# Moving a weight sum, four output copies and a pair of sums in a fused mLSTM and gated feed-forward kernel

## The chip, the cores and the metric

The kernel runs on one core of a Trainium2 chip. The metric is the device time of one execution in microseconds (us). The kernel before takes 461.69 us, the median of three runs that lie between 461.58 and 464.37.

The engines are named as the profile names them: PE is TensorE's matmul, PEld its weight load, DVE is VectorE, ACT is ScalarE, POOL is GpSimd and SP is SyncE, which here only issues DMAs. DMAs are also issued from ACT's queue and, for one chunk, from POOL's.

## The reference

An mLSTM cell with 4 batches, 8 heads, 768 time steps and a head size of 40 is followed by a feed-forward block over the 3072 tokens, from 320 to 2048 and back to 320, all in float32:

```
for t in range(S):
    m_new = np.maximum(f_gate[:, :, t] + m, i_gate[:, :, t])
    f_stab = np.exp(f_gate[:, :, t] + m - m_new)
    i_stab = np.exp(i_gate[:, :, t] - m_new)
    m = m_new
    C = f_stab[:, :, None, None] * C + i_stab[:, :, None, None] * np.einsum('bhd,bhe->bhde', vt, kt)
    n = f_stab[:, :, None] * n + i_stab[:, :, None] * kt
    h_tilde = np.einsum('bhde,bhe->bhd', C, qt)
    nq = np.einsum('bhd,bhd->bh', n, qt)[:, :, None]
    y[:, :, t] = sigmoid(o_gate[:, :, t]) * h_tilde / np.maximum(np.abs(nq), 1.0)
x = y.transpose(0, 2, 1, 3).reshape(B * S, H * D)
h = x @ w_in
g = h * (1.0 / (1.0 + np.exp(-1.702 * h)))
out = g @ w_out
```

(`vt`, `kt` and `qt` are the step's slices of v, k and q, and `sigmoid` stands for the expression written out.)

## The kernel before

**Chunks and stages.** The 768 steps are cut into six chunks of 128 (`w` = 0 to 5). A chunk's tokens are those of all four batches, 512 in all. For each chunk there is a first product (x by `w_in`, then the gate function) and a second product (by `w_out`). While the second product of chunk w runs on PE, the attention of chunk w + 1 is computed in between, block by block, so that its x is there when PE ends. Attention works on two halves, `c` = 0 and 1, of two batches each.

**The order of work is written out by hand.** There is no scheduler: each engine runs its instructions in the order in which the code issues them, and waits on semaphores where it reads what another engine or a DMA wrote.

**Fast products.** From chunk 1 on both products use a scheme with seven block products instead of eight, which needs sums of weights and of inputs. `weight_sums(0)` to `(3)` (line 811) make the sums of `w_out` once, on POOL, in place of room that chunk 0 used; sums 0 and 1 are issued at the end of chunk 0, sums 2 and 3 during the first product of chunk 1. `wait_for(x)` (line 596) is a copy of one column on POOL, whose only purpose is that POOL waits until `x` is written. `input_sums` (lines 673 to 676) make the sums of `w_in` on DVE, in two parts, after blocks 11 and 13 of chunk 0. `token_sums` (lines 684 to 689) make those of x on DVE, ahead of each fast first product.

**Chunk 0's second product** (`down`, line 798) is plain: 16 blocks of four products each, whose sums stay in four PSUM banks, one a batch. After blocks 9, 11, 13 and 15 a batch is complete: its bank is copied to `o_sb` (line 802) and stored by SP (line 803).

**The second product of chunks 1 to 5** (`down_fast`) has 14 blocks, 0 to 6 for the first half of the batches and 7 to 13 for the second. Each block is eight matmul pairs (line 852), and DVE copies or adds its bank to the outputs (lines 855 and 857). The last block of a half, and its third, read `total(2)`, a sum of gated inputs; between the two `last_sums` (line 837) changes each of its four parts in place on DVE. Parts 0 and 1 are changed behind the third block; parts 2 and 3 in the fifth block, ahead of that block's adds. In the last block the first four matmul pairs read parts 0 and 1, the others 2 and 3. Store 1 of a half goes to SP behind the sixth block's add, store 0 behind the last.

**Attention beside these blocks**, for the next chunk: weights (ACT line 439, POOL masks line 443), the state's carry (PE line 605, which needs `k_st`; DVE lines 583 and 616; POOL lines 592 and 583), scores (PE line 463, DVE line 466), values (PE lines 507 and 515) and `outputs` on DVE: lines 521 and 522, the denominator `den` (lines 473 to 475), and the gated outputs y (lines 477 and 482). `seam_out` writes y of a half to DRAM (`x_row` and `x_rest`, line 560; from SP for the first half, from ACT's queue for the second), `seam_in` fetches it back into `q_sq` (line 569, SP), and `seam_turn` transposes it into xT on DVE (line 576). Text below calls the transposes of the first half turn 0 and those of the second turn 1.

**Loads.** All inputs of a chunk are fetched one or two chunks ahead, in SP's queue: the squares of k and q (line 108) at block 13 (k) and 15 (q) of chunk 0 and at block 13 of later chunks, the gates' rows (lines 304 to 354), the weights' rows (line 407), and v and k (line 120). One DMA queue carries them in the order of issue.

Of the kernel before, what the change touches and what calls it, by code (L numbers as in the profile page):

```python
# [26 lines left out]
def kernel(  # L27
# [42 lines left out]
    V, A, G, T = nc.vector, nc.scalar, nc.gpsimd, nc.tensor  # L70
# [7 lines left out]
    t1, t2, t4 = (t_sb[:, i, :].rearrange("p (f m) -> p f m", m=DH) for i in range(3))  # L78
# [31 lines left out]
    def load(w, what, bs=slice(0, B)):  # L110
        hs = slice(bs.start * H, bs.stop * H)
        for c in what:
            if c == "o" and w not in eo:
                eo[w] = ld.tile([L, BH, D], FP, tag="eo", bufs=1, name="eo")
            dst, src = {"k": (k_of(w), k), "q": (q_st, q), "v": (v_st, v), "o": (eo.get(w), o_gate)}[c]
            if w and c in "kv":
                for i, t, r in ((0, slice(0, L), slice(0, L)), (1, slice(0, HL), slice(HL, L)),
                                (1, slice(HL, L), slice(0, HL))):
                    x = src[:, :, w * L + t.start:w * L + t.stop, :].rearrange("b (p two) s d -> two s (b p) d", two=2)
                    nc.sync.dma_start(out=dst[r, i::2, 0:D], in_=x[i])  # L120
                continue
            nc.sync.dma_start(out=dst[:, hs, 0:D],
                              in_=src[bs, :, w * L:(w + 1) * L, :].rearrange("b h s d -> s (b h) d"))
# [103 lines left out]
    kT, qT, ys, xT, gs, o_ps, sums, vw, x_row = {}, {}, {}, {}, {}, {}, {}, {}, {}  # L227
# [366 lines left out]
    def wait_for(x):  # L594

        G.tensor_copy(out=mark[0:x.shape[0]], in_=x[:, 0:1])
# [196 lines left out]
    def down(w, b, n):  # L793
        if n == 0:
            o_ps[w, b] = ps_m.tile([128, DM], FP, tag="m", name="p_out")
        po = o_ps[w, b]
        for f in range(n * 4, n * 4 + 4):
            T.matmul(po, gs[w, f // 2][:, f % 2, b * L:(b + 1) * L], w_out_sb[:, f, :], start=(f == 0),  # L798
                     stop=(f == NF - 1))
        if n == NF // 4 - 1:  # L800
            o = op.tile([128, DM], FP, tag="o", name="o_sb")
            V.tensor_copy(out=o, in_=po)
            nc.sync.dma_start(out=out[b * S + w * L:b * S + (w + 1) * L, :], in_=o)


# [3 lines left out]
    def weight_sums(n):  # L809
        out, a, b = ((t1, w01, w00), (t2, w11, t1), (w01, w11, w01), (t4, w10, t2))[n]  # L810
        G.tensor_tensor(out=out, in0=a, in1=b, op=OP.subtract)

    def hidden(w, j, b):

        return gs[w, j].rearrange("p i (c two t) -> p i c two t", two=2, t=L)[:, :, :, b, :]

    def hidden_difference(w, j):

        a00, a10 = hidden(w, j, 0), hidden(w, j, 1)
        G.tensor_tensor(out=a10, in0=a00, in1=a10, op=OP.subtract)  # L820
# [12 lines left out]
    def last_sums(w, c, js):  # L833

        for j in js:
            s2 = sums[w, 2, j // 2][:, j % 2, :, c]
            V.tensor_tensor(out=s2, in0=hidden(w, j + 4, 0)[:, :, c], in1=s2, op=OP.subtract)

    def down_fast(w, c):
        o = [op.tile([128, DM], FP, tag="o", name="o_sb") for _ in range(2)]  # L840
        o00, o01, o10, o11 = (o[i][:, n * DH:(n + 1) * DH] for i in range(2) for n in range(2))

        def block(two, k):
            return lambda f: gs[w, k * 4 + f // 2][:, f % 2, (2 * c + two) * L:(2 * c + two + 1) * L]

        def total(x):
            return lambda f: sums[w, x, f // 4][:, f // 2 % 2, f % 2, c, :]

        def product(a, b, *adds):
            po = ps_m.tile([128, DH], FP, tag="m", name="p_out")  # L850
            for f in range(NH):
                T.matmul(po, a(f), b[:, f, :], start=(f == 0), stop=(f == NH - 1))  # L852
            for dst, x in adds:
                if x is None:
                    V.tensor_copy(out=dst, in_=po)
                else:
                    V.tensor_tensor(out=dst, in0=x, in1=po, op=OP.add)  # L857

        def store(two):
            b = 2 * c + two  # L860
            nc.sync.dma_start(out=out[b * S + w * L:b * S + (w + 1) * L, :], in_=o[two])

        return [lambda: product(block(0, 0), w00, (o11, None)),
                lambda: product(block(0, 1), w10, (o00, o11)),
                lambda: (product(total(2), t2, (o01, o11)), last_sums(w, c, (0, 1))),
                lambda: product(block(1, 0), w01, (o10, o01)),
                lambda: (last_sums(w, c, (2, 3)), product(total(1), t1, (o11, o10), (o01, o01))),
                lambda: (product(block(1, 1), t4, (o10, o10)), store(1)),
                lambda: (product(total(2), w11, (o01, o01)), store(0))]


    def run(calls):
        for f, *args in calls:
            f(*args)
# [62 lines left out]
    for w in range(NW):  # L937
        more = w + 1 < NW
        if w == 0:
            for j in range(NF // 2):  # L940
                if j % 2 == 0:
                    ahead, behind = converted[j // 2]
                    run([(convert, p) for p in ahead] + [(fetch, p) for p in fetched.get(j // 2, ())])
                    up(w, j, lambda: run([(columns_turn, 1) if p is None else (convert, p) for p in behind]))
                if j == 6:
                    load(1, "o")
                if j == 1:
                    wait_for(w_in_sb[:, 1, 512:1024])
                    scale(0, 1)
                    load(1, "v")  # L950
                if j < B and j % 2:
                    carry(0, (j // 2,))
                if j == 3:
                    masks()
                    gates(1)
                    columns_in(1)
                if j == 4:
                    spread(1)
                    load_squares(1, "q")
                if j >= B:  # L960
                    transposes(1, j - B)
        else:
            token_sums(w)
            for j in range(NF // 2):
                up_fast(w, j)
                if more and j == 0:
                    gates(w + 1)
                    load(w + 1, "o")
                    if w == 1:
                        wait_for(ends[w + 1])  # L970
                if w == 1 and j < 2:
                    weight_sums(j + 2)
                if more and j == 2:
                    columns_in(w + 1)
                    spread(w + 1)
                    load(w + 1, "vk")
                if more and j:
                    for n in ((0, 2), (), (4,), (6, 1, 3), (5, 7), (), ())[j - 1]:
                        block_transposes(w + 1, n)
                if more and j == 7:  # L980
                    columns_turn(w + 1)
                if 2 <= j < 6:
                    hidden_difference(w, j - 2)
                if j >= 6:
                    hidden_sums(w, (j - 6,), G)
            gelu_fast(w, NF // 2 - 1)
            hidden_sums(w, (2, 3), V)
        side = attention(w + 1) if more else {}
        if w == 0:

            blocks = [(lambda b=b, n=n: down(w, b, n)) for n0 in (0, 2) for b in range(B) for n in (n0, n0 + 1)]
        else:
            blocks = down_fast(w, 0) + down_fast(w, 1)
        for i, block in enumerate(blocks):
            if w == 0 and i in (0, 4, 5):
                convert((17, 18, 19)[max(i - 3, 0)])
            if w + 2 < NW and i == (6 if w == 0 else 0):
                load_gates(w + 2)
            if w + 2 < NW and i == 13:
                load_squares(w + 2, "kq" if w else "k")  # L1000
            if w == 0 and i == 15:
                load_squares(w + 2, "q")
            block()
            run(side.get(i, []))
            if w == 0 and i == 3:
                for n in (1, 3, 5, 7):
                    block_transposes(1, n)
            if w == 0 and i == 6:
                wait_for(wt[1, 0][:, 0, 0, :])
                weight_sums(0)  # L1010
                weight_sums(1)
            if w == 0 and i in (11, 13):
                input_sums(slice(0, 4) if i == 11 else slice(4, 8))
# [30 lines left out]
```

## Time and profile before

| | |
|---|---|
| median of three runs | 461.69 us |
| the profiled execution, its time | 463.3 us |
| its span, first to last instruction | 461.6 us |
| PE busy | 452.8 us (98%) |
| PEld busy | 386.5 us (84%) |
| DVE busy | 350.9 us (76%) |
| ACT busy | 186.0 us (40%) |
| POOL busy | 162.7 us (35%) |
| mean granted TensorE clock | 1.000 |
| DMA | 52.87 MB, mean 115 GB/s |

The profile is of one execution, whose own time lies above its span by what is done before the first and after the last instruction. A row of a view in order of time has the start, the duration in us, the engine, the line of the code, the operation, what it writes and reads, its shape and the number of instructions merged; in brackets stands the idle time before it and what ended it. Where a row merges several instructions its duration is that of all of them. Instructions overlap a little at their ends, and matmuls, which are pipelined, more. Of the page's costliest groups these matter for the change:

```profile
L857 DVE TENSOR_TENSOR o_sb<-o_sb,p_out 128x160 f32<-128x160 f32 x70 | 21.4, 317 | 43.6 <-PE p_out L852 43.0
L768 ACT COPY parts<-p_h 128x256 f32<-128x256 f32 x40 | 14.9, 372 | 164.6 <-PE p_h L729 159.5
```

The columns are: line, engine, operation, out<-in, shapes and count; busy us and mean ns of one; idle time of the engine before them and what ended most of it. Two groups that the page leaves out are of interest too: `last_sums` (line 837) is 40 instructions of 609 ns on average, but 397 to 1505 each, and the copy of line 802 four instructions of 480 to 495 ns. `weight_sums` (line 811) is four instructions of some 2.9 us on POOL.

### The profile page before, as it was taken

To read this page: it belongs to the slowest core of one execution; us is meant where nothing else is said; L and a number is where in the kernel's file an instruction comes from. 1 tells how busy PE (TensorE), PEld (TensorE's weight loads), DVE (VectorE), ACT (ScalarE), POOL (GpSimd) and SP (SyncE) were. 2 spreads that over 40 slices of the span, in tenths; PEclk is the share of its full clock that TensorE was granted. 3 is DMA by queue.
4 is the path that set the end of the run, shared out by engine and by line. 5 is a ranking of instruction groups with operands and counts; after the bars stand their busy time and mean duration, and the time that the engine had idled before them with its cause. 6 is when DMAs were issued, how large, how long until landed. Compare 5 with 4: busy or idle time off the path is not lost.

```text
span 461.6 us, 12375 instructions
## 1 busy us (share of the span) xinstructions
PE 452.8 (98%) x5071; PEld 386.5 (84%) x5071; DVE 350.9 (76%) x738; ACT 186.0 (40%) x433; POOL 162.7 (35%) x155
## 2 busy tenths in 40 slices
PE   8999999999999999999899999999999999999996
PEld 6777877775779999779899779999888999787996
DVE  6788998899988876889786888787788767554622
ACT  5686779100546600546700354900264810164100
POOL 5101318130677500266700167610157710146200
PEclk9999999999999999999999999999999999999999
DMA  8999999038969044959224979315989505000000
GB/s 165 186 289 195 251 234 221 5 67 186 179 138 122 3 102 115 193 79 174 36 61 109 195 117 165 50 37 122 176 130 156 76 18 141 28 1 1 1 28 30
DMA packets 135561, 52.87 MB, mean 115 GB/s; under 512 B 101984, under 2 KB 131632, under 8 KB 135504
## 3 DMA queue, kind: packets, MB, share of 16 engines
q1 hardware_dynamic: 127136, 50.27, 56.0%
q10 hardware_dynamic: 8048, 1.66, 1.8%
q8 instruction: 40, 0.66, 0.7%
q0 software_dynamic: 320, 0.15, 0.2%
q14 instruction: 17, 0.14, 0.1%
HBM read 44.52 MB, written 7.54 MB: 113 GB/s over the span
## 4 chain that ended last, share of the span: by engine, by line
PE 75%; DVE 11%; ACT 4%; SPq 4%; DMA 3%; issue 2%; DVEq 0%; ACTq 0%
PE p_out L852 30%; PE p_h L729 16%; PE p_a L729 6%; PE p_h L631 5%; PE p_h L708 4%; PE p_a L708 3%; SPq L120 2%; PE p_a L507 2%; DMA st_row<-f_run 2%; PE p_a L515 2%; PE p_a L463 2%; PE p_a L605 2%; ACT wt L439 2%; PE p_h L640 1%; PE p_a L390 1%
## 5 line engine op out<-in xcount | busy, mean ns | idle before, releaser
L789 POOL TENSOR_TENSOR g<-g,parts 128x512 f32<-128x512 f32 x30 | 38.2, 1274 | 184.7 <-ACT g L746 175.9
L768 ACT COPY parts<-p_h 128x256 f32<-128x256 f32 x40 | 14.9, 372 | 164.6 <-PE p_h L729 159.5
L852 PE MATMUL p_out<-w_out_sb,g 128*128 128x160 f32 x480 | 68.9, 300 | 0.0
L852 PEld LDWEIGHTS p_out<-w_out_sb,g 128*128 128x128 f32 x480 | 66.4, 190 | 0.5
L697 ACT ACTIVATE g<-g 128x512 f32<-128x512 f32 x80 | 47.7, 629 | 23.8 <-DVE g L783 18.8
L857 DVE TENSOR_TENSOR o_sb<-o_sb,p_out 128x160 f32<-128x160 f32 x70 | 21.4, 317 | 43.6 <-PE p_out L852 43.0
L852 PE MATMUL p_out<-t_sb,s 128*128 128x160 f32 x320 | 47.1, 300 | 0.0
L729 PE MATMUL p_h<-xT,w_in_sb 128*128 128x256 f32 x160 | 45.4, 386 | 0.0
L852 PEld LDWEIGHTS p_out<-t_sb,s 128*128 128x128 f32 x320 | 44.4, 190 | 0.2
L729 PE MATMUL p_h<-t_x,s_in 128*128 128x256 f32 x160 | 41.2, 380 | 0.2 <-DVE t_x L684 0.2
L439 ACT ACTIVATE wt<-wt,cols 128x64 f32<-128x64 f32 x160 | 38.8, 333 | 0.1
L729 PEld LDWEIGHTS p_h<-xT,w_in_sb 128*128 128x128 f32 x160 | 29.4, 190 | 9.8 <-issue 6.3
L798 PE MATMUL p_out<-w_out_sb,g 128*128 128x320 f32 x128 | 35.7, 436 | 0.0
L729 PEld LDWEIGHTS p_h<-t_x,s_in 128*128 128x128 f32 x160 | 30.2, 190 | 4.8 <-DVE t_x L684 0.6
L798 PEld LDWEIGHTS p_out<-w_out_sb,g 128*128 128x128 f32 x128 | 23.9, 190 | 9.6
L769 DVE TENSOR_TENSOR t_x<-p_h,parts 128x256 f32<-128x256 f32 x40 | 17.0, 425 | 16.8 <-ACT g L697 8.7
L631 PE MATMUL p_h<-xT,w_in_sb 128*128 128x256 f32 x128 | 29.6, 384 | 0.0
L631 PEld LDWEIGHTS p_h<-xT,w_in_sb 128*128 128x128 f32 x128 | 23.6, 190 | 5.3 <-issue 2.4
L820 POOL TENSOR_TENSOR g<-g 128x512 f32<-128x512 f32 x20 | 25.5, 1276 | 0.0
L443 POOL TENSOR_SCALAR_AFFINE_SELECT wt<-wt 64x1024 f32<-64x1024 f32 x20 | 23.4, 1170 | 5.4 <-ACT wt L439 4.7
L852 PE MATMUL p_out<-w_out_sb,s 128*128 128x160 f32 x160 | 23.8, 302 | 0.0
L852 PE MATMUL p_out<-t_sb,g 128*128 128x160 f32 x160 | 23.8, 302 | 0.0
(221 smaller groups left out, 892.4 us busy)
## 6 DMA issues: line engine op xcount, KB each, us to landing
q_sq<-in_q_dram SPq DMA_DIRECT2D x20, 320.0 KB, 10.2
wt<-m_row SPq DMA_DIRECT2D x20, 256.0 KB, 5.6
k_sq<-in_k_dram SPq DMA_DIRECT2D x16, 320.0 KB, 6.3
out_dram<-o_sb SPq DMA_DIRECT2D x24, 160.0 KB, 1.9
eo<-in_o_gate_dram SPq DMA_DIRECT2D x5, 640.0 KB, 8.5
bits<-in_moe_w_in_dram SPq DMA_DIRECT2D x6, 512.0 KB, 11.4
q_sq<-x_row SPq DMA_DIRECT2D x10, 256.0 KB, 2.9
v_st<-in_v_dram SPq DMA_DIRECT2D x14, 160.0 KB, 5.9
```

Source lines behind the costliest of these rows:

```text
L439: A.activation(out=x[:, h, :], in_=x[:, h, :], func=AF.Exp, scale=-1.0, bias=cols[w][:, c * PH + h:c * PH + h + 1])
L443: G.affine_select(out=r, in_=r, compare_op=OP.is_ge, fill=0.0, base=0, pattern=[[0, PH], [1, HL]], channel_multiplier=-1)
L631: T.matmul(ph[j][i][:, t], w_in_sb[:, c, f * 128:(f + 1) * 128], x[:, c, t], start=(first and c == 0 and n == 0), stop=(not first and c == ...
L697: A.activation(out=gs[w, j][:, i, :], in_=gs[w, j][:, i, :], func=AF.Gelu_apprx_sigmoid)
L708: T.matmul(row[:, t], w_in_x[r, j, :], xT[w][r, 2].rearrange("p b t -> p (b t)")[:, t], start=(start and h == 0), stop=(not start and h == ...
L729: T.matmul(out, a, x[n], start=start, stop=stop)
L769: V.tensor_tensor(out=u2, in0=p56[:, right], in1=y[:, left], op=OP.add)
L789: G.tensor_tensor(out=g0, in0=g0, in1=u, op=OP.add)
L798: T.matmul(po, gs[w, f // 2][:, f % 2, b * L:(b + 1) * L], w_out_sb[:, f, :], start=(f == 0), stop=(f == NF - 1))
L820: G.tensor_tensor(out=a10, in0=a00, in1=a10, op=OP.subtract)
L852: T.matmul(po, a(f), b[:, f, :], start=(f == 0), stop=(f == NH - 1))
L857: V.tensor_tensor(out=dst, in0=x, in1=po, op=OP.add)
```

## The change

Three edits:

```diff
@@ down, chunk 0's second product
-            V.tensor_copy(out=o, in_=po)
+            A.copy(out=o, in_=po)
             nc.sync.dma_start(out=out[b * S + w * L:b * S + (w + 1) * L, :], in_=o)
@@ down_fast, the last three blocks of a half
-                lambda: (last_sums(w, c, (2, 3)), product(total(1), t1, (o11, o10), (o01, o01))),
-                lambda: (product(block(1, 1), t4, (o10, o10)), store(1)),
+                lambda: product(total(1), t1, (o11, o10), (o01, o01)),
+                lambda: (last_sums(w, c, (2, 3)), product(block(1, 1), t4, (o10, o10)), store(1)),
                 lambda: (product(total(2), w11, (o01, o01)), store(0))]
@@ the main loop, blocks of the second product
             if w == 0 and i == 6:
                 wait_for(wt[1, 0][:, 0, 0, :])
                 weight_sums(0)
+            if w == 0 and i == 8:
+                wait_for(ys[1, 0][:, 1, :])
                 weight_sums(1)
```

The four copies of chunk 0's outputs move from DVE to ACT; on ACT the first of them stands ahead of the four DMA issues of the second half's `seam_out`, the other three behind. On DVE nothing takes their place.

Parts 2 and 3 of the last sums move from the fifth block of a half to the sixth, in all five chunks with a fast product. On DVE they stand now behind whatever attention issues between these two blocks: the scores' two multiplications (line 466) in the first half, the four transposes of turn 1 in the second; and still ahead of the sixth block's add and its store.

The second weight sum stays on POOL and is the same instruction. It stood directly behind the first; now it is issued after block 8 and waits, by one more copy of a column, until the gated outputs of the first half of chunk 1 are written.

No instruction is dropped; one is added.

## The prediction

> **What bounds the kernel now.** I read the busy shares first, then TensorE's idle time by waiter, then stage lengths, then the order of time of the engines around each stage that is too long. The page's first part puts PE at 98% of a span of 461.6 us (DVE 76%, ACT 40%, POOL 35%), and the granted clock is 1.000 throughout. So work taken off another engine is worth only what it frees in a place where PE stands still.
>
> TensorE's waits (waiter, released by, us in total, times, longest):
> ```profile
> PE p_h L729 <- DVE xT L576: 0.9, 1, 0.9
> PE p_a L507 <- DVE wt L466: 0.7, 3, 0.3
> ...
> PE p_a L605 <- DMA k_st<-in_k_dram: 0.6, 1, 0.6
> ```
> The busy times by stage (window, length, busy and instructions of PE, PEld, DVE, ACT, POOL) say what these come to when the slowed matmuls around them are counted. The four first-product stages, chunks 1 to 4:
> ```profile
> 109.33:143.16 33.83, 32.80 (x147) 23.87 (x146) 29.92 (x62) 14.73 (x29) 21.11 (x16) 1.00 0.95 164
> 182.26:214.07 31.81, 31.81 (x146) 23.94 (x145) 27.91 (x57) 14.71 (x29) 15.31 (x13) 1.00 0.91 156
> ```
> and the second-product stages:
> ```profile
> 143.16:182.26 39.10, 38.90 (x738) 37.92 (x737) 29.63 (x65) 12.45 (x40) 11.37 (x10) 1.00 0.34 69
> 214.07:254.40 40.33, 39.14 (x738) 37.98 (x737) 30.08 (x65) 12.47 (x40) 11.40 (x10) 1.00 0.39 77
> ...
> 357.22:395.83 38.61, 38.61 (x673) 37.71 (x673) 26.72 (x61) 12.46 (x40) 11.10 (x10) 1.00 0.37 76
> ```
> Chunk 1's first product is 2.0 us over its likes (31.81 to 31.88); the second products of chunks 1 and 3 (39.10 each) are 0.5 over chunk 4's 38.61, and chunk 2's is 1.7 over. Some 4.7 us in all: nothing in this change can reach 1% of the time (4.6 us) unless it removes every one.
>
> **Part 1: second sum of weights and chunk 0's copies.** VectorE and GpSimd in order of time at the end of chunk 0:
> ```profile
> 93.30 2.90 POOL L811 TENSOR_TENSOR t_sb<-w_out_sb,t_sb 128x1280 f32<-128x1280 f32 x1
> 93.84 2.39 DVE L473 TENSOR_SCALAR den<-u 128x16 f32<-128x16 f32 x1
> ...
> 100.40 0.17 DVE L473 TENSOR_SCALAR den<-u 128x16 f32<-128x16 f32 x1
> ...
> 109.84 1.55 DVE L576 STREAM_TRANSPOSE xT<-q_sq 128x256 f32<-128x256 f32 x4
> ```
> The first L473 takes 2.39 us where its twin takes 0.17, and ends 0.03 after the second sum. Until turn 1 (the L576 at 109.84) ends, DVE is never idle, and PE's first product, begun at 109.33, waits for it: L708 starts at 114.35 in the chain, 5.02 us later, against 3.02 us (182.26 to 185.28) in chunk 2.
>
> Removed from DVE's path up to there: 2.39 - 0.17 = 2.2 us, and three copies of L802 at some 0.40 us of pitch (0.48 each, the next instruction starting 0.08 before its end), the fourth standing behind turn 1. Added again: the sum now starts when the first half's gated outputs are written. These end at 98.34 - 2.2 = 96.1; the marker copy and its start cost 0.15 to 0.6 us (it began 0.5 after the L466 it waited for, and took 0.14), so the sum runs from 96.3 to 99.2 at best, 96.7 to 99.65 at worst. The second half's L521 can't start before PE's L515 ends (96.4), so its L473 stands at 96.46 + 0.87 + 0.88 = 98.2 and is held 1.0 to 1.4 us. Its two L482 end 2.11 us after L473, at 101.4 to 101.8 instead of 102.68: of the 2.2 us, 0.9 to 1.3 arrive. Behind the new wait on GpSimd stands only L789 of the next stage, at 116.1.
>
> The Trainium skill ("SBUF — State Buffer", Who interferes with whom) states that VectorE and GpSimd hold a shared port pair exclusively for a whole instruction, the later one blocking fully. That speaks against putting the sum here, since by it the new place holds the next tensor_scalar as the old one did; were it wrong, DVE would be another 1.0 to 1.4 us earlier, and the sum below the same, as the next limits show.
>
> From 101.35 or 101.75 DVE has 2.53 us of input sums, turn 0 (1.40), 2.52 us of input sums again, and stands before turn 1 at 107.8 to 108.2. Turn 1 needs its DMAs too: the ACT queue issues x_row, SP fetches it back, and the last piece, issued at 106.92, landed 2.5 later, 6.7 us after the outputs. That gives 108.1 to 108.5. Turn 1 then ends at 109.4 to 109.9, and the token sums start there instead of at 111.61. PE, going through from 109.33 in its normal 3.02 us, asks for the first of them at 110.6 (ready 109.9 to 110.4) and for the last, x4 from L687, at 111.5 (ready 111.0 to 111.6). So PE loses at most 0.1 and gains 2.0; it can't start before 109.33, where block 15 ends, so the rest of DVE's gain is worth nothing.
>
> On ACT the four copies are costed at nothing: between the 256 and 512 column rows (372 and 581 ns) one is some 0.43 us, and ACT is idle from 83 to 102 and from 105 to 110. Queued behind the first is the issue of x_row for the second half, ready at 101; that copy runs at 98.2. The last one runs from 109.5 to 110.0, just ahead of L768, the copy of the next stage's first bank, which ran at 110.02; DVE wants L768's result at 112, so 1.5 us of cover remain. If that were gone, the price is one copy, 0.4. The four stores follow the copies on SP; the square loads behind them move 0.9 earlier with the fetch of x_row. The last k_st piece of chunk 2 landed at 149.08 for a product at 151.79, and moves to 148.2 for 149.8: cover 1.6.
>
> **Part 2: the last two sums one block later, first half.** In chunk 1, DVE in order of time:
> ```profile
> 156.28 2.26 DVE L837 TENSOR_TENSOR s<-g,s 128x256 f32<-128x256 f32 x2
> 158.47 0.54 DVE L857 TENSOR_TENSOR o_sb<-o_sb,p_out 128x160 f32<-128x160 f32 x2
> 158.93 2.34 DVE L466 TENSOR_TENSOR wt<-p_a,wt 128x1024 f32<-128x1024 f32 x2
> ```
> The pair of L837, 0.75 us elsewhere, takes 2.26 beside GpSimd's masks (L443, 155.86 to 158.28), and L466 behind it makes PE's L507 and L515 late: block 5 to block 6 is 4.84 us apart, against 4.38 in chunk 4. Moved, L857 runs at 156.3, the first L466 at 156.8, the second after the mask at 158.4 to 159.6; the products want them at 160.0 and 160.9. Chunk 3 shows the same rows. Gain 2 x 0.46 = 0.9. In chunks 2 and 4 L507 waits for nothing: gain 0. The sums themselves now end at 160.4, and the product that reads them (fifth matmul pair of block 6) comes at 163.
>
> **Second half.** Here the two sums go behind turn 1, and ahead of block 12's L857, whose store heads SP's queue:
> ```profile
> 178.54 1.56 DVE L576 STREAM_TRANSPOSE xT<-q_sq 128x256 f32<-128x256 f32 x4
> 180.12 0.32 DVE L857 TENSOR_TENSOR o_sb<-o_sb,p_out 128x160 f32<-128x160 f32 x1
> ```
> and SP's queue:
> ```profile
> 180.47 0.36 SPq L861 DMA_DIRECT2D out_dram<-o_sb  x1
> 180.88 2.08 SPq L108 DMA_DIRECT2D k_sq<-in_k_dram  x4
> ```
> L857 slips by 0.73 us (the pair's row at 177.42), and the store and eight loads of squares with it, in chunks 1, 2 and 3. What follows is one long queue of DMAs: from L108 at 180.88 to k_st's last landing at 223.5 is 42.6 us, and PE's L605 wanted it after 41.8; that is chunk 2's stall. The same stretch took 40.5 us in the next chunk and 41.1 in the one after. With 41.1 us allowed instead of 41.85, chunk 2 loses another 0.7, chunk 3 nothing (0.6 left), chunk 4 lies on the edge. I take 0.7; bounds 0 (another execution's DMAs as fast as chunk 3's; a gain is excluded, as nothing makes these loads start earlier against PE) and 3 x 0.73 = 2.2.
>
> Block 13 reads the moved sums from its fifth and seventh matmul pair on, at 181.2 and 181.7; they end at 180.5 and 180.9. Cost nothing, cover 0.6. In the last chunk nothing stands in the way, and the tail is the same.
>
> **The sum.** -2.0 - 0.9 + 0.7 = -2.2 us. The profiled execution took 463.3 us around its 461.6 of span, so 461.1; on the median of 461.69 (three runs, 461.58 to 464.37), 459.5.
>
> **Rivals.** (1) *The load queue binds in all three chunks*: for it, chunk 4's zero margin; against, chunk 3's 0.6. -2.9 + 2.2 = -0.7: 461.0. (2) *No chunk's queue binds*: the three stretches differ by 2 us between themselves, so chunk 2's may be chance. -2.9: 458.8. (3) *Part 1 gives nothing*: turn 1 still waits, for a transfer that doesn't move or a sum that holds DVE longer than worked out. For it, only 0.3 us lies between the landing and DVE; against, both move by 0.9 at least. -0.9 + 0.7: 461.5. (4) *Slower: block 13 waits for the moved sums.* They stand behind turn 1, and turn 1 behind its fetch, which in chunk 2 landed (247.72 + 2.9 = 250.6) no earlier than the transposes began (250.68). Once a fetch is over 0.6 us late, each further us holds block 13 by one, where the sums used to be done before. At 1 us beyond in each of chunks 1 to 4: +4.0 - 2.2 = +1.8: 463.5. (5) The change doesn't do what it says: a wait merged by the program onto block 13's first matmul would cost 0.9 x 4, giving 463.1; but in the built order the waits stand at the fifth and seventh pair.
>
> **How the numbers follow.** Forecast 0.52; (1) 0.14; (2) 0.17; (3) 0.07; (4) and (5) together 0.10, as nothing but a late fetch speaks for them. The time is the forecast's, 459.5. The range takes (2) with 0.4 of run-to-run play below, 458.4, and reaches past (1) and (3) to 461.9; 463 and over stays out. About 1% is what a measurement tells from no change. Below 457.1 every stall must go, chunk 2's too: 0.05. Above 466.3 needs (4) at over twice its price: 0.03. Within: 0.92.
>
> **What would show it.** Right: the L473 near 93.8 back at 0.17 and the one near 98.2 at 1.0 to 1.6; chunk 1's first product at 31.8 to 32.0; second products of chunks 1 and 3 at 38.6; chunk 2's at 41.0, with L605's wait for k_st near 1.3. Wrong: a wait of L852 for L837, or L729 still waiting for L576.

## The result and the profile after

The changed kernel takes 458.85 us, the median of five runs from 458.52 to 459.40. Beside it on the same chip the kernel before took 461.69. The ratio on record, which is not that of the two medians (0.9938), is 0.9929, with a 95% interval of 0.9916 to 0.9942: 0.7% faster, inside the band that was called no change, and the time is 0.65 us below the forecast of 459.5.

The profiled execution took 458.85 us, with a span of 457.1. The busy shares from the page:

```profile
span 457.1 us, 12380 instructions
...
PE 451.0 (99%) x5071; PEld 386.0 (84%) x5071; DVE 343.8 (75%) x734; ACT 187.3 (41%) x437; POOL 162.3 (36%) x156
```

TensorE's waits (waiter, released by, us in total, times, longest):

```profile
PE p_x L534 <- DVE y L482: 0.6, 1, 0.6
PE p_a L507 <- DVE wt L466: 0.6, 1, 0.6
```

The waits of L729 for L576 and of L605 for k_st are gone, and of L507's one is left, in chunk 0. The busy times by stage (the columns as in the prediction, then the clock, the DMA share and GB/s): the first product of chunk 1, then the second products of chunks 1, 2 and 3:

```profile
109.06:140.90 31.84, 31.84 (x146) 24.05 (x145) 27.28 (x57) 15.01 (x30) 20.97 (x16) 1.00 0.89 161
140.90:179.52 38.62, 38.62 (x737) 37.72 (x736) 28.46 (x65) 12.61 (x40) 11.46 (x10) 1.00 0.36 73
211.36:250.25 38.89, 38.85 (x738) 37.82 (x737) 29.08 (x65) 12.61 (x40) 11.37 (x10) 1.00 0.40 78
282.09:320.72 38.63, 38.63 (x738) 37.73 (x736) 28.47 (x65) 12.61 (x40) 11.41 (x10) 1.00 0.38 78
```

Each now stands at its likes (31.84; 38.61), but for 0.3 us in chunk 2. Stage lengths here and below run from the first matmul of a stage to the first of the next. So measured, they were 33.67 before for the first of these rows, and 39.10, 40.30 and 39.10 for the others. That is 1.83 + 0.48 + 1.41 + 0.47 = 4.2 of the 4.5 us by which the two spans differ. The medians differ by only 2.8. The runs below show that chance had a part in chunk 2's 1.41: it made the stage 1.2 us longer in the first profile of the kernel before, and 0.3 longer in this one.

**The end of chunk 0.** VectorE in order of time:

```profile
93.57 0.17 DVE L473 TENSOR_SCALAR den<-u 128x16 f32<-128x16 f32 x1
...
97.93 1.12 DVE L473 TENSOR_SCALAR den<-u 128x16 f32<-128x16 f32 x1
...
100.26 0.89 DVE L482 SCALAR_TENSOR_TENSOR y<-eo,den 128x320 f32<-128x320 f32 x2
...
107.53 1.55 DVE L576 STREAM_TRANSPOSE xT<-q_sq 128x256 f32<-128x256 f32 x4
108.94 0.40 DVE L684 TENSOR_TENSOR t_x<-xT 128x256 f32<-128x256 f32 x1
```

and GpSimd:

```profile
95.98 0.18 POOL L596 COPY mark<-y 128x1 f32<-128x1 f32 x1 [3.03 <-DVE y L482]
96.12 2.89 POOL L811 TENSOR_TENSOR t_sb<-w_out_sb,t_sb 128x1280 f32<-128x1280 f32 x1
```

The L473 of the first half is back at 0.17 us. That of the second, which took 0.17 before, takes 1.12 and ends 0.04 after the sum (96.12 + 2.89 = 99.01; 99.05). The token sums start at 108.94, 2.7 us earlier than before and before PE's first matmul of the stage (109.06).

**First half of a second product.** VectorE in chunk 1:

```profile
154.18 0.54 DVE L857 TENSOR_TENSOR o_sb<-o_sb,p_out 128x160 f32<-128x160 f32 x2
154.81 2.56 DVE L466 TENSOR_TENSOR wt<-p_a,wt 128x1024 f32<-128x1024 f32 x2
157.28 0.75 DVE L837 TENSOR_TENSOR s<-g,s 128x256 f32<-128x256 f32 x2
```

The two L837 now take 0.75 us together instead of 2.26. The two L466 end at 157.4, 16.5 us into the stage, where they ended 18.3 us into it before (158.93 + 2.34 - 143.00).

**Second half.** SP's queue in chunk 1:

```profile
178.25 0.36 SPq L861 DMA_DIRECT2D out_dram<-o_sb  x1
178.66 2.08 SPq L108 DMA_DIRECT2D k_sq<-in_k_dram  x4
```

From this L108 to the carry (L605) of the next chunk pass 41.49 us, where 41.84 passed before: the loads slip by 0.35 us against PE.

### The profile page after: what moved, and what is told of

Same layout as the page of the kernel before. It is cut to its first block, busy times and chain, and to the rows that moved or that the text cites. A ratio compares the mean times of both kernels' runs of the same rounds, so it can differ in the third digit from the quotient of the medians.

```text
span 457.1 us, 12380 instructions
## 1 busy us (share of the span) xinstructions
PE 451.0 (99%) x5071; PEld 386.0 (84%) x5071; DVE 343.8 (75%) x734; ACT 187.3 (41%) x437; POOL 162.3 (36%) x156
## 4 chain that ended last, share of the span: by engine, by line
PE 85%; DMA 7%; DVE 4%; SPq 1%; ACT 1%; issue 1%; DVEq 0%
PE p_out L852 34%; PE p_h L729 19%; PE p_a L729 8%; PE p_h L708 4%; PE p_a L708 4%; PE p_out L798 3%; PE p_a L507 2%; PE p_h L631 2%; DMA q_sq<-in_q_dram 2%; PE p_a L515 2%; PE p_a L463 2%; DMA fi<-in_f_gate_dram 2%; DMA bits<-in_moe_w_out_dram 2%; PE p_a L605 1%; DMA s_in<-in_moe_w_in_dram 1%; DVE qT L398 1%
## 5 line engine op out<-in xcount | busy, mean ns | idle before, releaser
L768 ACT COPY parts<-p_h 128x256 f32<-128x256 f32 x40 | 14.9, 372 | 135.0 <-PE p_h L729 135.0
L857 DVE TENSOR_TENSOR o_sb<-o_sb,p_out 128x160 f32<-128x160 f32 x70 | 21.5, 318 | 43.4 <-PE p_out L852 42.8
L729 PE MATMUL p_h<-xT,w_in_sb 128*128 128x256 f32 x160 | 45.4, 386 | 0.0
L729 PE MATMUL p_h<-t_x,s_in 128*128 128x256 f32 x160 | 41.1, 379 | 0.0
L729 PEld LDWEIGHTS p_h<-xT,w_in_sb 128*128 128x128 f32 x160 | 29.4, 190 | 9.8 <-issue 6.3
L729 PEld LDWEIGHTS p_h<-t_x,s_in 128*128 128x128 f32 x160 | 30.4, 190 | 4.1
```

What stands on the lines that cost most here:

```text
L729: T.matmul(out, a, x[n], start=start, stop=stop)
```

## The experiments

Unless a diff names the kernel before, it is against the changed kernel. Each ratio is to the kernel before, measured beside it on the same chip.

**1. The kernel before once more.** No edit.

> The kernel before, unchanged, profiled once more. Theory A (chunk 2's long second product in the first profile, 40.3 us, was the DMA transfers of that one execution): chunk 2's second product is 38.6 to 39.3 us, from the first square load of its queue to the last landing of k_st pass under 41.8 us, and the span is about 460. Theory B (the kernel before always waits there, and the change removed that wait): 40.2 to 40.5 us again, with TensorE's L605 released by k_st. Both: chunk 1's first product 33.7 to 33.9, second products of chunks 1 and 3 at 39.1; time within 0.2% of the kernel before.

462.05 us against 462.08, ratio 0.9998 (0.9988 to 1.0007). Its profiled span is 460.4, 1.2 us below the first. The difference is that of chunk 2's second product: 39.09 instead of 40.30. TensorE's waits:

```profile
PE p_a L507 <- DVE wt L466: 1.2, 4, 0.6
...
PE p_h L729 <- DVE xT L576: 0.9, 1, 0.9
```

No wait for k_st, and L507 waits four times instead of three. VectorE in chunk 2:

```profile
227.21 2.26 DVE L837 TENSOR_TENSOR s<-g,s 128x256 f32<-128x256 f32 x2
229.39 0.54 DVE L857 TENSOR_TENSOR o_sb<-o_sb,p_out 128x160 f32<-128x160 f32 x2
229.85 2.34 DVE L466 TENSOR_TENSOR wt<-p_a,wt 128x1024 f32<-128x1024 f32 x2
```

These are the rows of chunks 1 and 3. The profiles of experiments 2, 3 and 6, which leave the first half as it was, have 39.09 to 39.10 in chunk 2 as well. So the late load in the first profile belonged to that execution, and it hid that chunk 2 has the same stall as its neighbours.

**2 and 3. The two edits of part 1, each alone** (on the kernel before):

```diff
 # copies_only
-            V.tensor_copy(out=o, in_=po)
+            A.copy(out=o, in_=po)
 # sum_only
+            if w == 0 and i == 8:
+                wait_for(ys[1, 0][:, 1, :])
                 weight_sums(1)
```

> Only chunk 0's four copies go to ScalarE; the second weight sum stays directly behind the first, and the last sums stay in the fifth block. Theory A (the two edits of part 1 overlap, since TensorE can start no earlier than block 15 ends, and the transfer of the second half bounds turn 1): VectorE comes to turn 1 1.2 us earlier, and chunk 1's first product takes 32.0 to 32.3 us, nearly all of the 1.9 that both edits gave; time 1.5 to 1.8 us below before. Theory B (the weight sum's hold of 2.2 us on VectorE is the main part, and the edits' gains add): 33.0 to 33.4 us, time 0.5 to 0.8 below. Both: the first L473 takes 2.4 us again.

> Only the second weight sum goes behind the first half's gated outputs; the copies stay on VectorE. Theory A (overlap): the first L473 is 0.17, the second 1.0 to 1.2; VectorE comes to turn 1 1.1 us earlier, the fourth copy still stands behind it, and chunk 1's first product takes 32.2 to 32.6 us; time 1.2 to 1.6 us below before. Theory B (gains add): what the copies alone don't give of 1.9 us, so that the two runs' gains sum to 1.9.

Copies alone: 460.73, ratio 0.997 (0.996 to 0.998), chunk 1's first product 32.24. Sum alone: 461.03, ratio 0.9976 (0.9967 to 0.9986), first product 32.43. In time that is 1.35 and 1.05 us, a little less than either expectation. The gains in this stage are 1.43 and 1.24 us, 2.67 in sum, where both together give 1.83. They overlap, because VectorE's time before turn 1 counts only as far as PE waits for it.

**4, 5 and 6. The last sums**: both halves without part 1; the changed kernel with the move in the first half only; and the move in the second half alone, without part 1 or the first half's.

```diff
 # last_sums_first (last_sums_second: the same with c == 1 moved, on the kernel before)
-                lambda: product(total(1), t1, (o11, o10), (o01, o01)),
-                lambda: (last_sums(w, c, (2, 3)), product(block(1, 1), t4, (o10, o10)), store(1)),
+                lambda: (last_sums(w, c, (2, 3) if c != 0 else ()), product(total(1), t1, (o11, o10), (o01, o01))),
+                lambda: (last_sums(w, c, (2, 3) if c == 0 else ()), product(block(1, 1), t4, (o10, o10)), store(1)),
```

> Only the last two sums go one block later, in both halves. Theory A: second products of chunks 1 and 3 at 38.6 us (0.48 less each), chunk 2's between 38.6 and 39.3, time 0.9 to 1.0 us below before. Theory B (the later store holds the loads back, and chunk 2 pays): chunk 2's second product longer than in the kernel before's profile of the same call by 0.3 to 0.7 us, time 0.2 to 0.7 below. Both: chunk 1's first product 33.7 to 33.9.

> The changed kernel, but with the last two sums moved in the first half of each chunk alone. Theory A (the gain of this edit is all in the first half, and the later store of the second half costs nothing as long as the load queue has room): chunk 1's first product 31.8, second products of chunks 1 to 3 at 38.6 to 38.9 us, ratio to before 0.992 to 0.994, as the changed kernel. Theory B (the second half's move holds the loads back and costs something in most executions): 0.3 to 0.8 us faster than the changed kernel, ratio 0.9912 to 0.9922.

> The kernel before with the last two sums moved in the second half alone. Theory A: no stage changes by more than 0.05 us but for what the load queue's chance brings; block 12's store and the loads go out 0.3 to 0.4 us later against TensorE; ratio to before 0.999 to 1.001. Theory B (the later loads cost): second product of chunk 2 or 3 longer by 0.3 us or more, ratio 1.001 to 1.002.

Both halves alone: 460.69, ratio 0.9968 (0.9955 to 0.9981), with second products of 38.63 in all of chunks 1, 2 and 3 and the first product unchanged at 33.66; its 1.4 us are more than the 0.9 to 1.0 expected, since chunk 2 gains too. With the move in the first half only: 458.94, ratio 0.9932 (0.9917 to 0.9947), as the changed kernel. The second half alone: 462.04, ratio 1.0001 (0.9992 to 1.001), stages as before. The first half's move is worth 3 x 0.47 = 1.4 us; the second half's is worth nothing and, within 0.5 us, costs nothing.

**7 and 8. The loads of squares later and earlier**, in chunks 1 to 3:

```diff
 # loads_late: behind all of block 13
-            if w + 2 < NW and i == 13:
+            if w + 2 < NW and i == 13 and not w:
                 load_squares(w + 2, "kq" if w else "k")
...
             run(side.get(i, []))
+            if 0 < w < NW - 2 and i == 13:
+                load_squares(w + 2, "kq")
 # loads_early: a block sooner
+            if w + 2 < NW and i == (12 if w else 13):
```

> The changed kernel with the loads of squares of chunks 3 to 5 issued behind block 13 instead of ahead of it: 1.8 us later. Theory A (the load queue is within 0.1 to 2 us of holding TensorE, so that a shift of 0.35 us, which the change makes, is mostly hidden and one of 1.8 is not): stretches of 39.6 to 41.4 us against 39.7 allowed, so the second products of chunks 2, 3 and 4 grow by 0.2 to 2 us each, time 1.5 to 5 us above the changed kernel, ratio to before 0.996 to 1.004. Theory B (the queue has several us of room, and chunk 2's wait in the first profile had another cause): within 0.2% of the changed kernel, ratio 0.991 to 0.995.

> The changed kernel with these loads issued ahead of block 12's store, so that the four of k go out some 1.5 us earlier. Theory A: second products of chunks 1 to 3 at 38.6 us without a rest of a wait (the changed kernel's chunk 2 had 38.9), time equal to the changed kernel's or up to 0.3 us lower, ratio to before 0.992 to 0.993. Theory B (the queue isn't what made chunk 2 long): chunk 2's second product stays at 38.9 or above.

Late: 459.47 (458.72 to 460.76), ratio 0.9951 (0.9934 to 0.9969). The loads begin 1.8 us later against PE, and the median is some 0.6 us over the changed kernel's (two of five runs by 1.5 to 1.9), less than expected: the stretch itself, from the first L108 to the last landing of k_st, shortened to 38.4 and 39.8 us for chunks 2 and 3. The profiled execution is the fastest of its runs and shows a trace of the wait in chunk 3 only (L605 1.58 us instead of 1.44, the stage 38.86). Early: 458.76, ratio 0.9927 (0.9912 to 0.9942), all three chunks at 38.63, the time as the changed kernel's. The loads go out 4.4 us earlier against PE, not the 1.5 expected. So some 4 us more for the queue (the carry comes 45.9 us after the loads instead of 41.5) bring nothing in the median: the change's 0.35 us costs nothing there. That 1.8 us less cost something is likely, but the intervals overlap.

**9. The second sum behind the second half's outputs**, where it waits one block longer:

```diff
-            if w == 0 and i == 8:
-                wait_for(ys[1, 0][:, 1, :])
+            if w == 0 and i == 9:
+                wait_for(ys[1, 1][:, 1, :])
```

> The changed kernel with the second weight sum waiting for the second half's gated outputs instead of the first's. Theory A (GpSimd's sum holds any VectorE instruction with two SBUF inputs or a tensor_scalar on SBUF for what is left of its 2.9 us): the second L473 is back at 0.17, but one of the input sums L673 to L676 takes 2.5 to 3.6 us; turn 1 ends 1.5 to 2.2 us later than in the changed kernel, chunk 1's first product takes 32.6 to 33.4 us, time 0.8 to 1.6 us above it, ratio to before 0.9945 to 0.9965. Theory B (only the tensor_scalar of the denominator is held): nothing is held, turn 1 waits for its transfer, first product 31.8, time as the changed kernel.

459.98, ratio 0.9955 (0.9941 to 0.9970), chunk 1's first product 33.09. VectorE, then GpSimd:

```profile
98.89 0.17 DVE L473 TENSOR_SCALAR den<-u 128x16 f32<-128x16 f32 x1
...
101.81 3.40 DVE L674 TENSOR_TENSOR s_in<-s_in,w_in_sb 128x512 f32<-128x512 f32 x1
```

```profile
101.31 0.51 POOL L596 COPY mark<-y 128x1 f32<-128x1 f32 x1 [7.41 <-DVE y L482]
101.78 2.89 POOL L811 TENSOR_TENSOR t_sb<-w_out_sb,t_sb 128x1280 f32<-128x1280 f32 x1
```

L473 is free, and L674, 0.69 us in the changed kernel, takes 3.40. It ends 0.54 us behind the sum (101.78 + 2.89 = 104.67; 105.21), most of an L674 of its own. The sum takes its toll from whichever VectorE instruction of that kind comes in its time, and in the place that the change gives it a part of its time falls on L521 and L522, which took 0.84 us each as they do elsewhere. The price here is 2.7 instead of 0.95 us, and 1.1 us of the time.

**10. The changed kernel once more.** No edit.

> The changed kernel once more, beside the two others of this call. Theory A (gain = 1.83 at the end of chunk 0 + 0.47 in each of chunks 1, 2 and 3 = 3.2 us): ratio to before 0.9920 to 0.9940; second products of chunks 1 to 3 at 38.6 to 38.9 us. Theory B (chunk 2's 1.4 us in the first pair of profiles belongs to the change): 4.2 us, ratio 0.989 to 0.991.

458.85, ratio 0.9939 (0.9927 to 0.9952). Its profiled execution was the slowest of its runs (460.27), and shows in chunk 2 (40.10 us) what the first profile of the kernel before had shown. PE in order of time:

```profile
220.35 1.83 PE L605 MATMUL p_a<-vw,k_st 64*40 64x41 f32 x128
222.12 2.44 PE L852 MATMUL p_out<-t_sb,s 128*128 128x160 f32 x16
224.49 1.16 PE L463 MATMUL p_a<-qT,kT 40*64 40x64 f32 x64
226.51 1.16 PE L463 MATMUL p_a<-qT,kT 40*64 40x64 f32 x64 [0.86 <-DVE state L616]
```

L605 takes 1.83 us for 1.44, and the state that follows it is late for L463. In this execution k_st landed 41.85 us after the first L108, for a carry that begins after 41.48; in the first profile of this kernel it took 41.05. So the kernel before and the changed kernel both pay some 1.2 to 1.5 us here in some executions.

The 0.39 us of L605 are the smaller part. VectorE and GpSimd in the same chunk, and GpSimd's L592 in chunk 2 of the first profile of the changed kernel:

```profile
223.09 1.22 DVE L583 TENSOR_TENSOR state<-state_mid,cols 128x328 f32<-128x328 f32 x1
224.83 1.09 DVE L583 TENSOR_TENSOR state<-state_mid,cols 128x328 f32<-128x328 f32 x1
```

```profile
221.62 2.35 POOL L443 TENSOR_SCALAR_AFFINE_SELECT wt<-wt 64x1024 f32<-64x1024 f32 x2
224.44 2.49 POOL L443 TENSOR_SCALAR_AFFINE_SELECT wt<-wt 64x1024 f32<-64x1024 f32 x2 [0.47 <-ACT wt L439]
```

```profile
216.55 2.54 POOL L592 TENSOR_TENSOR vw<-v_st,cols 128x656 f32<-128x656 f32 x2 [2.68 <-DMA v_st<-in_v_dram]
```

The two L583 take 0.66 and 0.49 us in chunk 1; here each ends some 0.34 us behind one of GpSimd's masks (single masks, merged in the rows above, end at 223.97 and 225.57). GpSimd itself is late, because its L592 reads v_st, which the same queue brings ahead of k_st. Where nothing is late L592 starts 4.68 us into the stage. In this execution v_st landed 5.61 us into it and L592 began at 5.77; in the first profile of the kernel before it was 6.10 and 6.26. In the first profile of the changed kernel it was 5.04 and 5.20: there k_st was in time, but L583 took 0.96 us, and that is the 0.3 us by which chunk 2 was too long. So v_st runs late first, and a look at k_st alone misses it.

**11 and 12. Removing chunk 0's last wait.** In chunk 0 the L507 that still waits (0.6 us) stands behind an L466 that the conversion of `w_out`'s last tenth precedes. The conversion was put two blocks later; then, in a second kernel, the first sum as well, since it met the conversion:

```diff
 # convert_later (with loads_early's edit)
-            if w == 0 and i in (0, 4, 5):
-                convert((17, 18, 19)[max(i - 3, 0)])
+            if w == 0 and i in (0, 4, 7):
+                convert({0: 17, 4: 18, 7: 19}[i])
 # first_sum_later (that, and)
-            if w == 0 and i == 6:
-                wait_for(wt[1, 0][:, 0, 0, :])
+            if w == 0 and i == 7:
+                wait_for(w_out_sb[:, NF - 1, :])
                 weight_sums(0)
```

> The changed kernel with the loads of squares ahead of block 12's store, and with the last conversion of weights in chunk 0 (19) issued ahead of block 7 instead of block 5, so that the scores' multiplications L466 no longer stand behind it on VectorE. Theory A (TensorE's L507 in chunk 0 waits 0.6 us for L466 because of that conversion, and VectorE has 1.3 us idle behind L466): chunk 0's second product 0.5 to 0.7 us shorter than the 43.57 of the changed kernel, time 0.4 to 0.8 below it, ratio to before 0.9910 to 0.9925. Theory B (the conversion then holds the values' L521, and the wait moves there): second product within 0.2 us of 43.57, time as the changed kernel.

> As the kernel with the conversion ahead of block 7, and the first weight sum too goes later: it waits for that conversion instead of for the first scores. Theory A (in that kernel GpSimd's first sum, which starts behind the first L466, held the conversion's L256 for 2.4 us, and block 9 waited for it): L256 behind L466 takes 0.4 to 0.5 us, no wait of L798, chunk 0's second product 42.9 to 43.2 us, time 0.4 to 0.7 us below the changed kernel, ratio to before 0.9915 to 0.9930. Theory B (the conversion is simply too late behind L466): block 9 still waits 0.3 us or more, second product 43.5 or above, time not below the changed kernel.

The first missed; L507 no longer waits for L466, but another wait came: 459.70, ratio 0.9946 (0.9933 to 0.9960). Chunk 0's second product grew from 43.57 to 44.39. VectorE, and then the wait it made on PE:

```profile
88.61 2.79 DVE L256 TENSOR_SCALAR w_out_sb<-w_out_sb 128x512 f32<-128x512 f32 x1
```

```profile
PE p_out L798 <- DVE w_out_sb L265: 0.8, 1, 0.8
```

The first sum ran from 88.20 to 91.12, and L256, begun at 88.61, ended 0.28 behind it. With the sum behind the conversion L256 is 0.42 us and that stage 42.98. But the first sum now ends at 93.83 and holds an L473 too; VectorE in that kernel:

```profile
87.85 0.42 DVE L256 TENSOR_SCALAR w_out_sb<-w_out_sb 128x512 f32<-128x512 f32 x1
...
92.77 1.08 DVE L473 TENSOR_SCALAR den<-u 128x16 f32<-128x16 f32 x1
...
97.63 1.55 DVE L473 TENSOR_SCALAR den<-u 128x16 f32<-128x16 f32 x1
...
109.15 0.41 DVE L684 TENSOR_TENSOR t_x<-xT 128x256 f32<-128x256 f32 x1
```

PE begins the first product at 108.26, so L684 comes 0.89 us after it, and that product takes 32.32 instead of 31.84. Of the 0.59 us won, 0.48 are given back. The time is 458.54, ratio 0.9914 (0.9890 to 0.9938): the lowest median of all, but not told apart from the changed kernel's 0.9929 and 0.9939.

## Why the prediction was right in its range, and where a step failed

The time lies in the range, 0.65 us under the forecast. No errors cancelled: of the three terms -2.0, -0.9 and +0.7 the runs gave -1.83, -1.4 and nothing clear of noise, and the two larger misses go the same way. By these terms the time would be 458.5, 0.4 below what was measured; the profiled execution, whose time is the median, has 0.3 us of a late load in it (experiment 10). That the forecast looks no further off than 0.65 is partly a chance of the medians: in experiment 10 they differ by 3.27 us, here by 2.84.

**Part 1: right.** The second L473 was to be held 1.0 to 1.4 us after a latency of 0.15 to 0.6; it was held 0.95, after 0.13. Both edits together were to bring PE 2.0 us, through a stage back at its normal length; it brought 1.83 (the 33.83 read from the windows ended 0.16 past the stage). That PE, and not VectorE, sets what the edits bring is seen when the start of the first token sum (L684), counted from PE's first matmul of the stage, is set beside the stage's excess over 31.84, both in us:

| kernel | L684 after PE's start | excess |
|---|---|---|
| before | 2.28 | 1.83 |
| second sum behind second half | 1.63 | 1.25 |
| sum alone | 1.06 | 0.59 |
| first sum and conversion later | 0.89 | 0.48 |
| copies alone | 0.78 | 0.40 |
| conversion later | 0.19 | 0 |
| changed | -0.12 | 0 |

Each us costs a us beyond some 0.4, and nothing below it. The changed kernel has half a us in hand, which is why either edit alone gives most of the gain.

The Trainium skill ("SBUF — State Buffer", Who interferes with whom) states that VectorE and GpSimd share a port pair under an exclusive lock for a whole instruction; that a tensor_scalar can take it, in a mode that uses two ports; that an operation with two SBUF inputs contends with a GpSimd instruction that reads SBUF; and that one with at most one SBUF input, outside such modes, does not contend. The rows agree: L473 1.12 and L256 2.79 (tensor_scalar), L674 3.40 (two SBUF inputs), L521 and L522, which read one operand from PSUM, 0.84 beside the sum as without it. The profile doesn't say in which mode an instruction ran.

**The copies on ACT at nothing: right.** Each takes 0.43 us, as worked out; the last ends at 109.73, ahead of L768 at 109.75, which stands 0.69 us behind PE's first matmul of the stage as before (110.02 to 109.33).

**Part 2, first half: right in mechanism, too small by a chunk.** 0.48 and 0.47 in chunks 1 and 3, as worked out. The failed step is "In chunks 2 and 4 L507 waits for nothing: gain 0." Chunk 4 holds; chunk 2 gains the same 0.46, seen in the repeated profile of before and in the move alone (38.63 in all three). The term is 1.4, not 0.9.

**Part 2, second half: the step that failed.** The +0.7 for chunk 2's load queue was wrong: experiment 6 shows no cost of the later loads within 0.5 us, and the sign that was named, chunk 2 at 41.0 us with a wait of 1.3 for k_st, did not come (38.89, no such wait). Three things were wrong in it. The slip was taken as the pair's 0.73, as if L857 had followed turn 1 without a gap and turn 1 had stayed where it was. But the pair takes 0.65 from its start to that of L857 (177.26 to 177.91); L857 had begun 1.58 after turn 1 before, where L837 now begins 1.42 after it, so 0.16 were already lost there; and turn 1 begins 0.12 earlier against the stage's end (3.68 instead of 3.56 us ahead of it). That leaves 0.37, and 0.35 is what the loads show. Next, the 42.6 us of the queue, on which the term stood, were one execution's: in the two profiles of before and the two of the changed kernel the stretch to k_st's landing is 39.6 to 42.6 us over the same bytes, and passes the allowed 41.5 to 41.85 in one chunk of one execution of each. The page had a sign of it: the profiled execution took 463.3 us, 1.6 over the median of its runs, and chunk 2's second product was 1.2 over chunk 1's. A stall that only the profile's execution had can't be worsened, or removed, in the median. Last, "that is chunk 2's stall" named k_st alone: by the rows of experiment 10 a good part of it came by v_st, L592 and the masks that held L583. No run moved v_st alone. Rival (2), that no chunk's queue binds, came closest; its 458.8 needs -2.9, where the runs gave -1.83 - 1.4 = -3.2.

**Rivals (1), (3), (4), (5)** fell: chunk 3 never waited in the two profiles of the changed kernel; part 1 gave its 1.8; turn 1 was never late enough for block 13, and no wait was added on its first matmul.

**Open:** what makes the queue's stretch differ by 3 us between executions, how often the 1.2 to 1.5 us are paid, and whether loads that start 0.35 us later pay them more often. The single times (one of the changed kernel's five in experiment 10 at 460.27, none of the five in the result) are too few, and so are the profiles: chunks 1 to 3 show such a stall in two of the five kernels or repeats that begin the loads 0.35 us later, and in two of the five that begin them as before (one of these of 0.05 us).

## What to carry to other kernels

Set the profiled execution's time beside the median before a stall in it is priced: one that accounts for the excess may be that execution's own, and may hide a regular stall right behind it; a second profile of the unchanged kernel tells. Edits that shorten the same wait don't add up; measure how far the waiting engine's need lies behind the supply, and stop there. A GpSimd operation over SBUF is worth placing by what VectorE runs in its time: beside L521 and L522, which read PSUM, it was free; beside a tensor_scalar of 0.17 us it cost its whole remaining length.

## What was not expected of the hardware

An instruction of 0.17 us took 1.12 to 2.39, one of 0.42 took 2.79 and one of 0.69 took 3.40 beside a single GpSimd sum of 2.9 us. A held instruction ended after GpSimd's by its own free length less 0.13 to 0.15 us: L473 0.04 (free 0.17), L256 0.28 (0.42), L583 0.34 (0.49), L674 0.54 (0.69). It goes the other way too: the copy that GpSimd waited with began 0.13 us after VectorE's write and took 0.18 where VectorE left it alone, and 0.51 beside L673, 0.05 past its end. The same queued loads took 39.6 to 42.6 us from execution to execution.
